# The last group's output leaves in 9 transfers of 128 rows instead of 16 of 64, in a fused linear-attention and SwiGLU kernel

## The chip, the cores and the metric

The kernel runs on one core of a Trainium2 chip. The metric is the device time of one execution in microseconds, as the median of several runs; before the change it was 297.41 us, the median of three runs that lay between 297.12 and 297.60. The same inputs are used each time. Matrices are float32 in memory, multiplied as float16 and summed in float32.

## What is computed

The input is linear attention with 8 batches, 8 heads, 576 positions and 64 dimensions per head; its result is taken as 4608 tokens of 512 numbers each and goes through a gated feed-forward layer of width 1536.

```python
def _attn_ref(q, k, v):                       # each (8, 8, 576, 64)
    def phi(x):
        return np.where(x > 0, x, np.exp(x) - 1.0) + 1.0
    q_p, k_p = (phi(q), phi(k))
    kv = np.einsum('bhsd,bhse->bhde', k_p, v)
    z = np.sum(k_p, axis=2)
    num = np.einsum('bhsd,bhde->bhse', q_p, kv)
    den = np.einsum('bhsd,bhd->bhs', q_p, z)[..., None] + 1e-06
    return (num / den).astype(np.float32)

def _moe_ref(x, w_gate, w_val, w_out):        # x (4608, 512), w_gate and w_val (512, 1536), w_out (1536, 512)
    g = x @ w_gate
    silu = g * (1.0 / (1.0 + np.exp(-g)))
    val = x @ w_val
    return (silu * val @ w_out).astype(np.float32)
```

Between the two, x is attn_out.transpose(0, 2, 1, 3) reshaped to (4608, 512).

## The kernel before

**Groups and tokens.** The 4608 tokens are worked off in 9 groups of 512, g = 0 to 8. A group is 8 units of 64 tokens. A unit (b, j) holds the positions 9c + j of batch b, for c = 0 to 63; so the rows of one unit lie 9 rows apart in `out`, and two units j and j + 1 lie beside each other. The last group, g = 8, is batch 7 with j = 1 to 8. A partition of an output tile is a token: the tile `osb[2 * th + tt]` holds two units, one in partitions 0 to 63 and one in 64 to 127. There are four such tiles, (th, tt) in {0, 1} x {0, 1}; below, `o0.0`, `o1.0`, `o2.1` and so on mean `osb` tile and column half (256 of the 512 columns).

**Layer 1** (lines 351 to 380) makes `hT`, the hidden activations in float16, on TensorE (PE), with ScalarE (ACT) for copies and Silu and VectorE (DVE) for products. **Layer 2** multiplies `hT` by `w_out`. From group 1 on, both use a scheme with seven block products in place of eight. In layer 2 each half tt of a group's tokens has the products 1 to 7, each 6 matmuls of 128 x 128 by 256 columns (`prd`, L456, line of the matmul). Sums of `hT` that products 3, 5, 6 and 7 need are made by DVE (`h_sum`, L425, tiles `hs`). The results are put together out of PSUM by `keep` (ACT, L465, PSUM to `part`), `copy_half` (ACT, L461) and `fin` (DVE, L470: PSUM times a constant plus `part`, into `osb`). Of one half tt, with o1 = `osb[tt]` and o2 = `osb[2 + tt]`:

- product 1 goes to bank x, and `keep` takes it to `part0`; product 2 goes to bank z, and `fin` makes the left columns of o1;
- product 6 is added in x and kept in `part1`; product 5 is added in z and kept in `part2`;
- product 7 is added in x, and `fin` with `part2` makes the right columns of o2;
- product 3 is added in z, and `fin` with `part1` makes the right columns of o1;
- product 4 is added in x, and a copy makes the left columns of o2. For the last group's tt = 1 this copy is a `tensor_scalar` on DVE (L997).

Bank x is `pX[tt]`, bank z is `(pX[2], pV[2])[tt]`. `seed_bank(tt)` is `(pV[1], pG[1])[tt]`, a bank that layer 1 uses; a switch `SEED[g]`, false for all groups, could send product 2 there.

**The order of the work.** For groups 1 to 8 nothing is issued where it is written. `op(engine, cost, function, reads, writes)` records an operation, `ORDER[g]` gives the order of the layer 2 products of a group ("51e" is product 5 of tt = 1, its first five matmuls; "51d" the sixth), and at the end a list of numbers written out in full decides the order in which all recorded operations are issued (an engine works off its own operations in that order):

```python
    for i in steps.split():
        ops[int(i)][2]()
```

The second argument of `op` is a planner's cost and has no effect on the device.

**The output.** Groups 1 to 7 write whole rows: `put` issues two transfers per tile on the queue of SyncE (SP), each 64 rows of 2 KB. The last group writes each column half as soon as it is done, `out_op` with two transfers of `put_1` (L1014), one per unit: 64 rows of 1 KB, that is 64 KB. These are 16 transfers: 13 issued by SP, 2 by ACT and 1 by GpSimd (POOL). The DRAM side of `put_1` picks one j, so it is 64 rows that lie 9 rows apart; the on-chip side is 64 partitions.

Of the kernel before, what the change touches and what calls it, by code (L numbers as in the profile page):

```python
# [13 lines left out]
P = 128  # L14
# [3 lines left out]
def kernel(  # L18
# [414 lines left out]
    def l2_banks(tt):  # L433
        return (pX[0], pX[1])[tt], (pX[2], pV[2])[tt]
# [4 lines left out]
    def prd(g, n, tt, fs, seeded):  # L439
# [15 lines left out]
        for (i, f) in enumerate(fs):  # L455
            nc.tensor.matmul(out=(z if n in (2, 3, 5) else x)[:, 0:HD], lhsT=left(f), rhs=right(f),  # L456
                             start=(i == 0 and fs[0] == 0 and (n in (1, 5) or n == 2 and not seeded)),
                             stop=(i == len(fs) - 1), skip_group_check=True)
# [9 lines left out]
    def fin(tt, th, ch, i, from_x):  # L468
        (x, z) = l2_banks(tt)
        nc.vector.scalar_tensor_tensor(out=osb[2 * th + tt][:, HD * ch:HD * ch + HD],  # L470
                                       in0=(x if from_x else z)[:, 0:HD], scalar=1.0 / SC, in1=part[:, 2 * i + tt, :],
                                       op0=ALU.mult, op1=ALU.add)
# [484 lines left out]
    def l2_prd(g, n, tt, fs=tuple(range(HF)), done=True):  # L957
# [11 lines left out]
        if n == 1:  # L969
            if sd:  # L970
                op("ACT", 0.3, lambda: copy_half(x, seed_bank(tt)[:, 0:HD], 1.0), [nm(x)], [nm(seed_bank(tt))])
            else:
                op("ACT", 0.3, lambda: keep(tt, 0, True), [nm(x)], [f"part0{tt}"])
        if n == 2:
            if sd:
                op("ACT", 0.3, lambda: copy_half(dst, o1[:, 0:HD], 1.0 / SC), [nm(dst)], [f"o{tt}.0"])
            else:
                op("DVE", 0.34, lambda: fin(tt, 0, 0, 0, False), [nm(z), f"part0{tt}"], [f"o{tt}.0"])
# [6 lines left out]
        if n == 7:  # L985
            op("DVE", 0.34, lambda: fin(tt, 1, 1, 2, True), [nm(x), f"part2{tt}"], [f"o{2 + tt}.1"])
            if last:
                out_op(g, tt, 1, 1, (nc.sync, nc.scalar) if tt else (nc.sync, nc.sync))
        if n == 3:
            op("DVE", 0.34, lambda: fin(tt, 0, 1, 1, False), [nm(z), f"part1{tt}"], [f"o{tt}.1"])  # L990
            if last:
                out_op(g, tt, 0, 1, (nc.sync, nc.gpsimd) if tt else (nc.sync, nc.sync))
            else:
                op("SP", 0.12, lambda: put(g, tt, 0), [f"o{tt}.0", f"o{tt}.1"], [])
        if n == 4:
            if last and tt:
                op("DVE", 0.34, lambda: nc.vector.tensor_scalar(out=o2[:, 0:HD], in0=x[:, 0:HD], scalar1=1.0 / SC, scalar2=None,  # L997
                                                                op0=ALU.mult), [nm(x)], [f"o{2 + tt}.0"])
                out_op(g, tt, 1, 0, (nc.sync, nc.scalar))
# [7 lines left out]
    def out_op(g, tt, th, ch, engs=(nc.sync, nc.sync)):  # L1007
        for e in range(2):
            eng = {id(nc.sync): "SP", id(nc.scalar): "ACT", id(nc.gpsimd): "POOL"}[id(engs[e])]
            op(eng, 0.06, lambda e=e: put_1(g, tt, th, ch, e, engs[e]), [f"o{2 * th + tt}.{ch}"], [])  # L1010

    def put_1(g, tt, th, ch, e, eng):
        (b, j) = units(g)[2 * (2 * th + tt) + e]
        eng.dma_start(out=out[S * b:S * b + S, HD * ch:HD * ch + HD].rearrange("(c j) f -> j c f", j=J)[j],  # L1014
                      in_=osb[2 * th + tt][C * e:C * e + C, HD * ch:HD * ch + HD])
# [122 lines left out]

    def program():
# [21 lines left out]
        0 1 4 14 15 9 17 18 10 5 20 21 23 6 24 26 27 16 29 3 19 30 32 8 2 33 35 36 7 22 38 28 41 25 39 40 42 31  # L1161
        34 44 45 43 37 47 63 46 48 64 49 105 66 12 50 67 69 106 65 70 51 11 72 68 73 52 75 71 13 76 114 78 77 79
        74 81 80 82 84 53 83 85 54 87 86 88 90 55 89 91 107 93 56 94 92 96 95 57 97 99 98 100 58 102 59 101 103
        113 127 104 60 129 108 128 109 131 117 171 133 110 132 130 135 112 115 137 134 139 111 136 125 138 120
        141 116 143 119 142 145 140 118 122 147 146 144 150 124 126 148 153 121 162 151 156 61 165 155 154 123
        168 62 149 152 163 167 158 176 164 157 172 177 169 159 179 166 170 178 160 181 161 197 180 342 199 182
        200 343 183 198 202 184 204 201 206 203 174 207 185 209 208 205 211 186 210 214 215 173 212 218 220 219
        213 222 175 221 187 223 225 216 224 227 217 229 228 188 230 285 226 232 231 189 234 236 235 237 233 240
        242 238 241 245 243 246 239 248 190 247 250 244 249 252 251 253 276 255 191 254 257 256 259 277 192 258
        193 260 262 261 264 194 267 265 268 263 271 266 273 269 272 274 270 284 298 275 300 278 280 299 302 279  # L1170
        301 286 281 304 303 282 306 288 308 305 287 310 307 296 309 289 312 283 314 313 311 316 290 291 318 317
        315 293 321 319 324 322 297 292 333 326 336 294 325 334 195 339 327 328 347 329 196 320 348 504 323 340
        335 338 350 330 341 337 349 331 352 368 332 353 370 354 369 371 355 373 372 375 356 295 377 357 378 380
        379 376 382 381 358 385 386 351 383 389 344 387 391 393 390 392 394 374 384 396 359 398 397 388 400 360
        399 401 395 403 456 405 402 404 407 345 408 406 411 409 413 346 412 361 416 410 414 417 419 415 418 421
        364 423 422 424 420 426 425 362 428 430 429 447 431 363 365 448 427 433 432 435 438 436 439 434 442 437
        444 440 443 445 441 455 469 446 471 449 470 450 473 457 451 475 452 474 472 477 459 476 479 453 478 481
        467 480 454 462 483 458 485 484 460 487 482 464 486 489 488 498 461 491 501 490 366 468 492 505 499 493
        367 507 494 500 506 496 510 508 495 512 466 502 463 515 503 509 517 497 513 465 516 523 514 518 525 519
        511 527 529 524 528 540 526 542 541 545 543 531 547 546 629 550 530 552 548 551 554 532 553 556 544 558  # L1180
        555 561 557 559 563 562 549 566 560 564 568 567 570 565 569 533 572 571 574 573 577 620 579 575 578 582
        580 576 584 534 586 583 588 585 587 590 589 593 581 591 595 594 598 621 521 600 596 602 601 603 599 535
        606 592 604 608 607 611 597 605 612 609 520 614 613 615 536 617 616 522 618 628 610 642 537 619 644 622
        643 624 646 632 623 648 625 626 645 650 635 647 652 649 627 654 651 653 637 656 633 658 634 657 660 655
        700 630 662 661 671 659 663 640 631 674 664 672 641 666 667 677 665 675 679 636 678 682 668 680 684 639
        669 670 687 638 689 688 701 694 538 685 691 696 690 702 683 539 698 673 676 681 686 706 695 703 715 697
        699 717 716 704 720 707 722 721 725 718 708 705 727 726 723 729 728 731 709 719 733 730 736 732 734 738
        737 724 741 739 743 742 745 710 804 744 747 735 749 746 752 748 750 754 753 740 757 755 751 759 758 761
        711 756 763 760 762 765 764 768 712 770 766 769 773 713 693 775 771 777 714 778 767 776 781 774 779 783
        782 772 786 780 784 787 692 789 797 788 790 792 798 791 793 785 803 815 795 794 817 796 816 819 799 807  # L1190
        800 821 820 801 818 823 805 825 822 802 827 824 826 810 829 808 831 871 830 806 833 828 812 832 835 834
        844 872 836 809 847 837 845 838 873 850 846 839 852 840 848 851 855 841 849 853 842 857 814 843 854 860
        874 862 811 861 865 858 875 864 867 813 859 863 856 869 876 882 866 891 870 868 893 892 877 896 894 884
        898 897 901 880 883 903 902 905 895 899 907 904 909 906 908 900 912 910 914 913 917 885 911 915 919 918
        921 886 916 923 920 887 922 925 924 928 878 930 929 933 926 879 881 935 934 931 937 936 888 939 927 938
        941 944 940 889 932 946 890 945 942 949 951 947 950 953 979 952 955 954 943 957 960 980 956 962 948 961
        958 965 968 963 959 969 966 971 972 970 967 974 964 973 975 977 978 981 976 989 990 991 992 993 983 996
        982 998 1000 997 1002 984 1004 999 985 1011 994 1003 1006 1001 1013 988 995 1015 987 1014 1007 1017 1012
        1016 986 1005 1019 1047 1018 1021 1008 1020 1023 1009 1022 1026 1024 1028 1010 1027 1025 1048 1031 1029
        1033 1049 1032 1030 1036 1034 1050 1038 1037 1035 1051 1041 1039 1052 1043 1042 1040 1045 1053 1044 1060  # L1200
        1046 1062 1061 1065 1056 1067 1066 1070 1063 1072 1068 1071 1074 1073 1054 1076 1064 1078 1075 1055 1057
        1081 1077 1079 1083 1082 1069 1086 1080 1084 1088 1087 1090 1058 1092 1089 1094 1091 1093 1059 1097 1095
        1099 1098 1085 1102 1096 1100 1104 1103 1106 1101 1108 1105 1107 1110 1109 1148 1113 1111 1115 1114 1118
# [43 lines left out]
```

## Time and profile before

The profile is of one execution of this kernel. Its own time was 297.82 us; the span from the first to the last record is 296.0 us, and 1.82 us lie around it.

| What | Value |
|---|---|
| median of three runs | 297.41 us (297.12 to 297.60) |
| profiled execution, span | 297.82 us, 296.0 us |
| PE busy | 286.4 us, 97% |
| DVE busy | 258.6 us, 87% |
| ACT busy | 236.3 us, 80% |
| POOL busy | 42.5 us, 14% |
| granted PE clock | 0.998 |
| last matmul of the program starts | 289.76 us |
| last copy out of PSUM | 290.07 to 290.49 us |
| last output issue on SP starts | 292.65 us |
| last output transfer has landed | 294.66 us |
| end of the span | 296.0 us |

How to read it: times are microseconds from the start of the span. PE, DVE, ACT and POOL are engines with their busy time; PEld is TensorE's loading of weights, which runs beside its matmuls. A line of the timeline gives start, duration, engine, line of the kernel, operation, output and inputs, shape and how many; instructions that follow each other closely are drawn together, so the duration is that of the group. SPq, ACTq and POOLq are the instructions of an engine that issue transfers; they aren't counted as busy. A bracket at the end of a line gives idle time before it and what ended it. In the DMA view a queue's line gives packets, megabytes and the time that the packets took, as a share of 16 DMA engines over the window; a transfer's line gives where from and to, who issued it, how many, the size of one and the median time from issue to landing.

### The profile page before, as it was taken

Reading aid. Unit: us, or ns where it says so; the run is one execution under the profiler, and the core shown is the slowest. Engines: PE = TensorE matmul, PEld = TensorE weight load, DVE = VectorE, ACT = ScalarE, POOL = GpSimd, SP = SyncE. Lnnn points to the kernel's source line nnn. Section 1 sums busy time; section 2 is a strip of 40 time slices with the busy share of each in tenths; the row PEclk is TensorE's granted clock in tenths of the full one; section 3 lists DMA queues with packets and bytes.
Section 4 is the critical chain, followed back from the end, with each engine's and each line's share of the span. In section 5 each row is a group of like instructions: output and inputs, shape, how many; then the busy total and the mean of one; then the engine's idle time right before and its main releaser. Section 6 shows DMA issues by size and latency. Waiting matters only on the chain.

```text
span 296.0 us, 7377 instructions
## 1 busy us (share of the span) xinstructions
PE 286.4 (97%) x2939; PEld 212.9 (72%) x2939; DVE 258.6 (87%) x521; ACT 236.3 (80%) x405; POOL 42.5 (14%) x55
## 2 busy tenths in 40 slices
PE   7899999999999999999999999999999999999991
PEld 5644454454866687668887888788888888788881
DVE  4667889999999998999899999999999999757961
ACT  4773977983998689969999999999986688668830
POOL 8554436500000011000100010000000000000000
PEclk9999999999999999999999999999999999999999
DMA  7999999995598319661960669304140443050014
GB/s 203 193 196 200 205 207 207 196 216 87 81 171 190 64 15 171 162 105 33 147 181 2 105 98 222 61 2 100 44 73 2 99 95 22 2 129 15 0 41 103
DMA packets 41506, 32.92 MB, mean 111 GB/s; under 512 B 16432, under 2 KB 36848, under 8 KB 41472
## 3 DMA queue, kind: packets, MB, share of 16 engines
q0 software_dynamic: 20176, 18.35, 40.7%
q1 hardware_dynamic: 21136, 13.97, 21.0%
q8 instruction: 23, 0.38, 0.5%
q10 hardware_dynamic: 160, 0.13, 0.2%
q14 instruction: 11, 0.09, 0.1%
HBM read 37.75 MB, written 9.44 MB: 159 GB/s over the span
## 4 chain that ended last, share of the span: by engine, by line
issue 50%; PE 43%; DMA 2%; ACT 2%; POOL 1%; POOLq 0%
PE pV L826 7%; PE pX L456 6%; PE pG L826 6%; PE pX L351 5%; PE pX L297 3%; PE pV L297 3%; DMA q<-in_q_dram 2%; PE pG L383 2%; PE pV L383 2%; PE pG L297 2%; PE pV L456 2%; PE pX L826 1%; PE pX L268 1%; PE pV L351 1%; PE pX L187 1%
## 5 line engine op out<-in xcount | busy, mean ns | idle before, releaser
L351 PEld LDWEIGHTS <-wl 128*128 128x128 f16 x414 | 40.3, 98 | 9.6 <-issue 0.2
L456 PEld LDWEIGHTS <-hs 128*128 128x128 f16 x384 | 37.2, 98 | 5.4 <-issue 0.7
L456 PEld LDWEIGHTS <-hT 128*128 128x128 f16 x288 | 27.7, 98 | 5.1 <-DVE hs L425 0.4
L351 PEld LDWEIGHTS <-wg 128*128 128x128 f16 x272 | 26.4, 98 | 5.7
L456 PE MATMUL pX<-ws,hs 128*128 128x256 f16 x240 | 28.8, 273 | 0.1
L826 PE MATMUL pV<-xt,wv 128*128 128x512 f16 x104 | 28.3, 379 | 0.0
L368 ACT ACTIVATE ek<-eq 128x512 f16<-128x512 f32 x34 | 21.3, 625 | 5.3 <-DVE eq L855 5.2
L351 PE MATMUL pV<-xt,wg 128*128 128x256 f16 x168 | 23.9, 273 | 0.0
L826 PE MATMUL pG<-xt,wg 128*128 128x512 f16 x80 | 22.5, 379 | 0.0
L368 ACT ACTIVATE ek<-pV 128x512 f16<-128x512 f32 x34 | 20.3, 597 | 2.7 <-PE pV L351 1.9
L351 PE MATMUL pX<-xs,wl 128*128 128x256 f16 x132 | 19.8, 273 | 0.0
L465 ACT ACTIVATE part<-pX 128x256 f32<-128x256 f32 x40 | 14.3, 386 | 6.4 <-PE pX L456 6.3
L456 PE MATMUL pX<-wo,hT 128*128 128x256 f16 x144 | 19.0, 273 | 0.0
L371 DVE SCALAR_TENSOR_TENSOR r<-pG,rr 128x512 f16<-128x512 f32 x20 | 13.7, 687 | 5.5 <-PE pG L351 5.2
L374 DVE SCALAR_TENSOR_TENSOR hT<-pV,sil 128x512 f16<-128x512 f32 x26 | 17.6, 684 | 0.9 <-PE pV L826 0.3
L425 DVE TENSOR_TENSOR hs<-hT 128x512 f16<-128x512 f16 (+3 forms) x35 | 17.8, 514 | 0.0
L365 ACT ACTIVATE rr<-pX 128x512 f32<-128x512 f32 x27 | 15.9, 598 | 2.4 <-PE pX L351 2.3
L470 DVE SCALAR_TENSOR_TENSOR osb<-pX,part 128x256 f32<-128x256 f32 x32 | 12.9, 419 | 5.2 <-ACT part L465 2.9
L1014 POOL DMA_DIRECT2D out_dram<-osb x1 | 0.6, 562 | 116.8 <-DVE osb L470 116.8
L249 DVE TENSOR_TENSOR qp<-qp,rden 128x768 f16<-128x768 f16 (+3 forms) x19 | 17.2, 906 | 0.0
L826 PEld LDWEIGHTS <-wv 128*128 128x128 f16 x112 | 10.9, 98 | 8.5
L124 ACT ACTIVATE ek<-k 128x1152 f16<-128x1152 f16 x14 | 16.1, 1161 | 1.3 <-DMA k<-in_k_dram 1.3
(187 smaller groups left out, 725.2 us busy)
## 6 DMA issues: line engine op xcount, KB each, us to landing
out_dram<-osb SPq DMA_DIRECT2D x64, 128.0 KB, 2.9
k<-in_k_dram POOLq DMA_DIRECT2D x7, 576.0 KB, 7.4
q<-in_q_dram POOLq DMA_DIRECT2D x7, 576.0 KB, 8.9
v<-in_v_dram POOLq DMA_DIRECT2D x7, 576.0 KB, 6.3
wg<-in_moe_w_gate_dram POOLq DMA_DIRECT2D x5, 256.0 KB, 9.2
wv<-in_moe_w_val_dram POOLq DMA_DIRECT2D x5, 256.0 KB, 9.8
wo<-in_moe_w_out_dram POOLq DMA_DIRECT2D x2, 512.0 KB, 15.1
out_dram<-osb SPq DMA_DIRECT2D x13, 64.0 KB, 2.1
```

What stands on the lines that cost most here:

```text
L124: nc.scalar.activation(out=e[:, s, :], in_=src[ix(b)][:, s, :], func=AF.Exp, bias=0.0, scale=1.0)
L249: nc.vector.tensor_tensor(out=qv, in0=qv, in1=rden[:, HL * j0:HL * j1].unsqueeze(2).to_broadcast([P, HL * (j1 - j0), D]), op=ALU.mult)
L297: nc.tensor.matmul(out=ps[:, :], lhsT=src[:, i, P * fb:P * fb + P], rhs=xT[i][g % 2][:, :], start=(i == 0), stop=(i == 3))
L351: nc.tensor.matmul(out=dst[:, HN * e:HN * e + HN], lhsT=lhs, rhs=rhs, start=(n in (1, 5) and e == 0 and c == 0), stop=(c == 1), skip_group ...
L365: nc.scalar.activation(out=dst, in_=halves(src), func=AF.Copy, bias=0.0, scale=scale)
L368: nc.scalar.activation(out=dst, in_=src, func=AF.Silu, bias=0.0, scale=1.0)
L371: nc.vector.scalar_tensor_tensor(out=dst, in0=halves(src), scalar=SC, in1=b, op0=ALU.mult, op1=op1)
L374: nc.vector.scalar_tensor_tensor(out=hT[:, fb, :], in0=pv[:, :], scalar=SC, in1=s[:, :], op0=ALU.mult, op1=ALU.mult)
L425: (eng or nc.vector).tensor_tensor(out=o, in0=a, in1=b, op=op)
L456: nc.tensor.matmul(out=(z if n in (2, 3, 5) else x)[:, 0:HD], lhsT=left(f), rhs=right(f), start=(i == 0 and fs[0] == 0 and (n in (1, 5) or ...
L465: nc.scalar.activation(out=part[:, 2 * i + tt, :], in_=(x if from_x else z)[:, 0:HD], func=AF.Copy, bias=0.0, scale=1.0 / SC)
L826: nc.tensor.matmul(out=dst[:, :], lhsT=src[:, i, P * fb:P * fb + P], rhs=xT[i][g % 2][:, :], start=(i == 0), stop=(i == 3))
```

## The change

The change touches the end of layer 2 and the order of the work.

1. **Transfers.** The eight column halves of the last group are now written with one transfer each of both units, 128 partitions, in place of two of 64; the DRAM side picks two neighbouring j, so it is 2 times 64 rows. Only the last, the left half of `osb[3]`, is written in two transfers of 128 columns (512 B a row). That makes 9: seven on SP, two on ACT (`o3.1` and the second part of `o3.0`), none on POOL.
2. **The last copy** (product 4 of tt = 1) is split: DVE copies the first 128 columns, ACT the other 128, and each half has its own transfer, DVE's on SP and ACT's on ACT.
3. **The last group's products** come in another order (`ORDER[8]`), and with `SEED[8] = 2` product 2 goes to the bank `seed_bank(tt)`, from which `fin(own=True)` reads it; there is no copy of product 1 into that bank.
4. **The list `steps`** is replaced as a whole. PE's operations are the same up to the 490th of 507 (509 after). Of DVE's 421 operations 243 stand at another place in its own order, of ACT's 358 (359 after) 129, over all groups. SP's order differs only in the last group, and the loads are as before.

```diff
             nc.tensor.matmul(out=(z if n in (2, 3, 5) else x)[:, 0:HD], lhsT=left(f), rhs=right(f),
-                             start=(i == 0 and fs[0] == 0 and (n in (1, 5) or n == 2 and not seeded)),
+                             start=(i == 0 and fs[0] == 0 and (n in (1, 5) or n == 2 and seeded is not True)),
...
-    def fin(tt, th, ch, i, from_x):
+    def fin(tt, th, ch, i, from_x, own=False):
         (x, z) = l2_banks(tt)
+        if own:
+            z = seed_bank(tt)
...
         if n == 1:
-            if sd:
+            if sd is True:
...
         if n == 2:
-            if sd:
+            if sd is True:
...
-                op("DVE", 0.34, lambda: fin(tt, 0, 0, 0, False), [nm(z), f"part0{tt}"], [f"o{tt}.0"])
+                op("DVE", 0.34, lambda: fin(tt, 0, 0, 0, False, sd == 2), [nm(dst), f"part0{tt}"], [f"o{tt}.0"])
...
-                out_op(g, tt, 1, 1, (nc.sync, nc.scalar) if tt else (nc.sync, nc.sync))
+                out_op(g, tt, 1, 1)
...
-                out_op(g, tt, 0, 1, (nc.sync, nc.gpsimd) if tt else (nc.sync, nc.sync))
+                out_op(g, tt, 0, 1)
...
         if n == 4:
             if last and tt:
-                op("DVE", 0.34, lambda: nc.vector.tensor_scalar(out=o2[:, 0:HD], in0=x[:, 0:HD], scalar1=1.0 / SC, scalar2=None,
-                                                                op0=ALU.mult), [nm(x)], [f"o{2 + tt}.0"])
-                out_op(g, tt, 1, 0, (nc.sync, nc.scalar))
+                hd = HD // 2
+                op("DVE", 0.2, lambda: nc.vector.tensor_scalar(out=o2[:, 0:hd], in0=x[:, 0:hd], scalar1=1.0 / SC, scalar2=None,
+                                                               op0=ALU.mult), [nm(x)], [f"o{2 + tt}.0a"])
+                op("ACT", 0.2, lambda: nc.scalar.activation(out=o2[:, hd:HD], in_=x[:, hd:HD], func=AF.Copy, bias=0.0,
+                                                            scale=1.0 / SC), [nm(x)], [f"o{2 + tt}.0b"])
+                op("SP", 0.06, lambda: put_1(g, tt, 1, 0, 0, 2, nc.sync, 0, hd), [f"o{2 + tt}.0a"], [])
+                op("ACT", 0.06, lambda: put_1(g, tt, 1, 0, 0, 2, nc.scalar, hd, HD), [f"o{2 + tt}.0b"], [])
...
-    def put_1(g, tt, th, ch, e, eng):
-        (b, j) = units(g)[2 * (2 * th + tt) + e]
-        eng.dma_start(out=out[S * b:S * b + S, HD * ch:HD * ch + HD].rearrange("(c j) f -> j c f", j=J)[j],
-                      in_=osb[2 * th + tt][C * e:C * e + C, HD * ch:HD * ch + HD])
+    OUTQ = {(0, 0, 0): "S", (0, 0, 1): "S", (1, 1, 0): "S", (0, 1, 0): "S", (1, 0, 0): "S", (1, 1, 1): "A", (0, 1, 1): "S"}
+    QUEUE = {"S": ("SP", nc.sync), "A": ("ACT", nc.scalar), "P": ("POOL", nc.gpsimd)}
+
+    def out_op(g, tt, th, ch):
+        qs = OUTQ[(th, ch, tt)]
+        for (i, x) in enumerate(qs):
+            e0, e1 = (0, 2) if len(qs) == 1 else (i, i + 1)
+            op(QUEUE[x][0], 0.06, lambda x=x, e0=e0, e1=e1: put_1(g, tt, th, ch, e0, e1, QUEUE[x][1]), [f"o{2 * th + tt}.{ch}"], [])
+
+    def put_1(g, tt, th, ch, e0, e1, eng, c0=0, c1=HD):
+        (b, j) = units(g)[2 * (2 * th + tt) + e0]
+        eng.dma_start(out=out[S * b:S * b + S, HD * ch + c0:HD * ch + c1].rearrange("(c j) f -> j c f", j=J)[j:j + e1 - e0],
+                      in_=osb[2 * th + tt][C * e0:C * e1, HD * ch + c0:HD * ch + c1])
...
-    ORDER[8] = "10c 20c 11c 21c 10d 20d 11d 21d 60 61 50 70 30 40 51 71 31 41"
+    ORDER[8] = "10c 11c 20c 21c 10d 11d 50e 20d 21d 60 61 51e 50d 51d 70 71 30 40 31 41"; SEED[8] = 2
```

## The prediction

> **What bounds the kernel now.** I read the page first, then the timeline of the last 15 us, the queue of SP (SyncE) alone, the waits, and the DMA view in small windows.
>
> ```profile
> span 296.0 us, 7377 instructions
> ...
> PE 286.4 (97%) x2939; PEld 212.9 (72%) x2939; DVE 258.6 (87%) x521; ACT 236.3 (80%) x405; POOL 42.5 (14%) x55
> ```
>
> TensorE (PE) is busy for 286.4 of 296.0 us, and from group 1 on its matmuls follow each other at their own length. So VectorE (DVE) and ScalarE (ACT) cost nothing while PE never waits for them. What is left is the tail. Timeline of 281 to 296 us (start, duration, engine, line):
>
> ```profile
> 282.76 0.27 PE L456 MATMUL pV<-wo,hT 128*128 128x256 f16 x1
> 283.17 2.78 PE L456 MATMUL pX<-ws,hs 128*128 128x256 f16 x24
> ...
> 283.80 9.40 SPq L1014 DMA_DIRECT2D out_dram<-osb  x13
> ...
> 285.79 0.82 PE L456 MATMUL pX<-wo,hs 128*128 128x256 f16 x6
> ...
> 286.52 0.81 PE L456 MATMUL pX<-ws,hT 128*128 128x256 f16 x6
> ...
> 290.07 0.42 DVE L997 TENSOR_SCALAR osb<-pX 128x256 f32<-128x256 f32 x1 [0.31 <-PE pX L456]
> ```
>
> 24 matmuls in 2.78 us, the last 0.27 long, are 0.109 apart. From 282.76 to 283.17 is 0.41: a stall of 0.30. Six start at 285.79, so the next was due at 286.44 and came at 286.52: 0.08, and the same again at 289.22 (after 288.49). PE loses 0.46 in the tail. The last copy ends at 290.49, and then SP still has a backlog:
>
> ```profile
> 289.85 3.36 SPq L1014 DMA_DIRECT2D out_dram<-osb  x5
> ```
>
> ```profile
> 292.02 1.19 SPq L1014 DMA_DIRECT2D out_dram<-osb  x2
> ```
>
> These are two windows of the same queue, from 289.8 and from 292.1 us: five issues fill 289.85 to 293.21, and the last starts at 292.65 (293.21 less 0.55), 2.16 after its data. The DMA view of 283 to 296 us (packets, MB, share of 16 engines; then issues, size, median time to landing):
>
> ```profile
> q1 hardware_dynamic: 1040, 0.85, 29.0%
> ...
> out_dram<-osb SPq DMA_DIRECT2D x13, 64.0 KB, 2.1
> ```
>
> The last issue lands 2.0 later, at 294.66; SP's final semaphore waits and drains take 1.33 more, to 296.0. The profiled execution took 297.82, the median of three runs is 297.41. Changes of the span are added to the median; about 0.6 us (0.2%) is what a measurement tells from no change.
>
> **The copies and products (small).** The reordered list puts the first five matmuls of product 5 between the last matmuls of products 1 and 2, and gives products 3 and 4 of a half at least one other product after the `fin` that frees their bank: the three stalls go, −0.46, next late is nothing on PE. Product 2 now goes to a seed bank, whose last reader is the Silu at 280.61 to 281.19; the product starts at 281.12 but that Silu now runs ahead of its neighbour, so I cost it at nothing, 0.07 without that cover. The last copy takes 0.42 for 256 columns; 512 columns take 0.684 (L371), so 128 take about 0.29 (ACT, 0.384 and 0.597: 0.28): −0.13. Both halves read one PSUM bank; no row shows two engines reading one bank together, so ACT's half costs 0 to 0.29 more. The ACT-issued transfer of `o3.1` waits for `fin` of product 7; ACT's next copies queue behind it, but that `fin` ends about 1 us before the copy of product 4 could start.
>
> **The planner's order (groups 1 to 8).** PE's order is the same up to its 490th operation of 507; of 421 DVE operations 243 stand elsewhere, of ACT's 129 of 358. For each I summed the trace durations of what moved ahead of it, less what moved behind, and set this against the time from its end to its PE user's start. 19 places overrun, by 5.5 us in all; that is the upper end. The lower is −0.33, PE's stalls there beyond a fixed 0.09 at each change of matmul shape; the largest:
>
> ```profile
> 211.62 0.60 PE L351 MATMUL pV<-xs,wl 128*128 128x256 f16 x4
> 211.63 0.31 PEld L351 LDWEIGHTS <-wl 128*128 128x128 f16 x3 [0.23 <-issue]
> ```
>
> It waits for the ACT copy at 210.99, now moved ahead of the Silu at 210.47, so −0.22. Overruns mostly vanish when walked, as here in group 8:
>
> ```profile
> 269.99 0.60 ACT L368 ACTIVATE ek<-pV 128x512 f16<-128x512 f32 x1 [0.33 <-PE pV L351]
> 270.62 0.58 ACT L365 ACTIVATE pV<-pG 128x512 f32<-128x512 f32 x1
> 271.12 0.62 ACT L368 ACTIVATE ek<-eq 128x512 f16<-128x512 f32 x1
> ```
>
> The last one moves ahead of the other two, 0.52 more in front, but ACT idles 0.33 before 269.99 and waits for PE at 270.62: 269.58 + 0.52 + 0.50 is 270.60, no shift. I take −0.22, nearest to this row.
>
> **The transfers (large).** Nine instead of sixteen: SP issues 7, ACT 2, POOL none. Seven move 128 rows of 1 KB, two 128 rows of 512 B. If they spread like today's, SP's issue stays near 0.55 (the page's first loads, 256 rows, issue as fast) and the backlog goes. But the pattern is new: in DRAM a transfer's outermost step is now j, of length 2, with 64 rows inside; it was 64 rows flat. In the DMA view above 1040 packets are 13 times 80: 64 rows and 16 completions, so sixteen engines take four rows each. The first two loads (window 1.5 to 6.0 us) are outermost 128:
>
> ```profile
> q1 hardware_dynamic: 544, 1.18, 75.6%
> ```
>
> 544 is twice 256 rows and 16 completions. So every outermost length that the trace shows is a multiple of 16 and was dealt over 16 engines. No row shows a length of 2. Two ends: 16 engines, 8 rows each; or two slices, two engines, 64 rows each. I take the second: slices of the outermost step are all that the trace shows being dealt out.
>
> The Trainium skill, "DMA: Bandwidth & Descriptors", section "Why a DMA increments its semaphore by 16 and not by 1", speaks against this change: it says the engines used are the largest number up to 16 that divides the slowest dimension of both sides, which would be 2 here; and that a transfer with fewer takes the lowest-numbered ones, so they would queue; by it the two-engine sum below holds, and by a spread over 16 the fast rival's. No run here shows a length of 2 yet.
>
> The price of a row: sixteen engines at once, 29.0% of 16 times 13 us is 60.3 us for 832 rows, 0.072 each. One engine alone (window 287.42 to 287.56, two rows and a completion):
>
> ```profile
> q1 hardware_dynamic: 3, 0.00, 4.6%
> ```
>
> 4.6% of 16 times 0.14 us is 0.103: 0.034 to 0.052 a row. Two engines are nearest to the lone one; a completion carries almost nothing, so 0.048. A full transfer is 64 times 0.048, 3.07 per engine; seven are 21.5. A half-wide one is 1.5 to 3.1, I take 2.3, two are 4.6. Sum 26.1, on the same two engines if a transfer always takes the first ones. DVE finishes `o0.0` 0.80 later than today (behind `o1.0`'s `fin` and an `hs` sum: 284.16 instead of 283.36), so the first issue is at 284.6, and bytes move 1.1 later (283.80 to about 284.95 now): 285.7. Queued work keeps both engines busy from there: 285.7 + 26.1 = 311.8, landing 0.4 later (2.0 less 1.1 and 0.46 of moving), end 1.33 later: span 313.55, +17.55. 297.41 + 17.55 = 315.0. All gains on PE are hidden under this queue. An issue that finds an engine occupied holds its queue (SP, one issue of 1.59 from 285.60), so SP's and ACT's issues should stretch to about 3 us; ACT has two copies behind its first, but nothing that the engines would not serve later anyway.
>
> Ends: 0.034 a row and half of it for half rows gives 17.4, 306.2; 0.072 and full price for half rows gives 41.3, 330.
>
> **Rivals.**
>
> *Faster: sixteen engines.* It decides if a pattern of outermost length 2 is dealt over all sixteen; break-even lies at about six engines: 26.1 on each of two is 52.2 us of engine time, and from 285.7 to 294.26 (today's last landing less 0.4) are 8.6 us. Then the last copy ends at 290.49 − 0.46 − 0.22 − 0.13 = 289.68; SP is held until 289.81 by `o1.1`'s issue (ready 289.16, 0.03 and 0.60); 2.0 and 0.15 for the extra rows per engine (four rows of 0.072 at most) give 291.96 against 294.66: −2.7, 294.7. If issues of 128 rows take double, +1.1: 295.8. For it: every transfer so far used sixteen. Against it: none had this pattern. 0.17.
>
> *Faster, a little: two engines, others each time.* Then the transfers don't queue behind each other, and the last whole one decides: `o1.1`, ready at 289.16, bytes from 290.3 for 3.07, landed 0.4 later, at 293.8 against 294.66: 296.5. Against it: with sixteen of sixteen in every row, nothing shows a rotation. 0.04.
>
> *Two engines at the shared price.* 0.072 a row, up to 330; against it, only two engines draw on memory at once. 0.07.
>
> *New stalls.* Sixteen engines and all overruns real: 294.7 + 0.2 + 5.5 = 300.4. Against it the ACT rows above. 0.03.
>
> *The split does not split.* If ACT's half waits for DVE's, its transfer starts up to 0.29 later: the fast case becomes 294.9. This moves no sign.
>
> **How the numbers follow.** Two engines at 306 to 330: 0.76 (0.07 of it the shared price). Faster: 0.21, sixteen engines (0.17) and the rotation (0.04), 294.3 to 296.5. New stalls that eat the gain: half within 0.2%, half slower, 0.03 together. So faster 0.21, same 0.02, slower 0.77. The likeliest case's own range is 306 to 324. The range must reach the faster case: 294.5 to 320 holds about 0.2 of the fast ones, 0.03 of the stalls and 0.6 of the slow one.
>
> **What would show it.** Per transfer 130 packets (128 and 2 completions) in the two-engine case, 144 for sixteen; the DMA digits after PE's end at 1 (2 of 16) for some 20 us, or at 5 and more for 2 us; landing after many us, or 2.2; SP issues of 3 us, or 0.55. PE's last matmul should start at about 289.1 in either case, unless ACT is held at its issue early enough to stop PE. Wrong would be: 144 packets, an idle DMA tail, or an end that PE sets.

## The result, and the profile after

The changed kernel takes 312.1 us (median of 4 runs, 311.76 to 312.25) against 297.5 us for the kernel before (median of 4 runs, the three from before the change among them): a ratio of 1.049, interval 1.047 to 1.051. The profiled execution took 311.76 us with a span of 309.9 us. The head of its page:

```profile
span 309.9 us, 7365 instructions
...
PE 286.4 (92%) x2939; PEld 213.1 (69%) x2939; DVE 258.8 (84%) x521; ACT 235.6 (76%) x406; POOL 42.7 (14%) x54
```

TensorE is as busy as before, 286.4 us, in a span that is 13.9 us longer: no engine works noticeably more, something is waited for at the end. Two windows of SP's queue in the timeline, from 283 us and from 290.1 us, then 288 to 296 us of the timeline, and ACT's two issues in the view of the line that issues (shortest, median and longest in ns):

```profile
283.87 18.06 SPq L1024 DMA_DIRECT2D out_dram<-osb  x7
```

```profile
290.16 11.77 SPq L1024 DMA_DIRECT2D out_dram<-osb  x3
```

```profile
288.56 0.29 DVE L1000 TENSOR_SCALAR osb<-pX 128x128 f32<-128x128 f32 x1 [0.23 <-PE pX L456]
288.89 0.28 ACT L1002 ACTIVATE osb<-pX 128x128 f32<-128x128 f32 x1 [0.79 <-DVE osb L1000]
289.20 0.53 ACTq L1024 DMA_DIRECT2D out_dram<-osb  x1
```

```profile
L1024 ACTq DMA_DIRECT2D out_dram<-osb x2: 527/832/1137, 286.5 to 289.2; - x2
```

The last copy has ended at 289.17, 1.3 us earlier than before (290.49). But SP, at that moment, is still in its fourth issue; the last three take 11.77 us, 5.08, 3.48 and 3.02 each, where one took 0.55 before. The span ends 20.7 us after the last copy. The DMA view of 283 to 310 us:

```profile
DMA  0101111111111111111111111111111111111000
GB/s 0 24 0 27 35 27 47 47 47 49 41 18 49 49 47 49 49 49 49 47 46 46 47 47 46 47 49 49 47 49 49 49 49 49 49 43 44 28 0 0
...
q1 hardware_dynamic: 910, 0.85, 9.4%
q10 hardware_dynamic: 260, 0.20, 2.4%
```

A digit of 1 stands for 10 to 20% of 16 engines, and two of 16 are 12.5%: two engines for 23 us, at about 48 GB/s. 910 packets on SP's queue are 7 times 130, 260 on ACT's are 2 times 130: 128 rows and 2 completions, where before 80 were 64 rows and 16 completions. The first row starts at 285.08, the last ends at 308.46, the span 1.44 later.

### The profile page after: what moved, and what is told of

Its sections match the earlier page's. It is cut to its first block, busy times and chain, and to the rows that moved or that the text cites. A ratio compares the mean times of both kernels' runs of the same rounds, so it can differ in the third digit from the quotient of the medians.

```text
span 309.9 us, 7365 instructions
## 1 busy us (share of the span) xinstructions
PE 286.4 (92%) x2939; PEld 213.1 (69%) x2939; DVE 258.8 (84%) x521; ACT 235.6 (76%) x406; POOL 42.7 (14%) x54
## 4 chain that ended last, share of the span: by engine, by line
PE 82%; DMA 10%; POOL 1%; issue 0%; DVE 0%; ACT 0%; POOLq 0%
PE pX L456 19%; PE pV L351 13%; PE pG L351 11%; PE pX L351 9%; PE pV L828 8%; PE pG L828 6%; PE pV L456 5%; DMA wo<-in_moe_w_out_dram 4%; DMA wv<-in_moe_w_val_dram 3%; DMA v<-in_v_dram 3%; PE pV L383 2%; PE pG L383 2%; PE pX L828 2%; PE pX L187 1%; PE pG L268 1%; PE pV L268 1%
## 5 line engine op out<-in xcount | busy, mean ns | idle before, releaser
L456 PE MATMUL pX<-wo,hT 128*128 128x256 f16 x138 | 18.2, 273 | 0.0
L351 PE MATMUL pG<-xs,wl 128*128 128x256 f16 x100 | 16.9, 272 | 0.0
L368 ACT ACTIVATE sil<-pG 128x512 f16<-128x512 f32 x20 | 11.9, 593 | 5.4 <-PE pG L828 4.7
```

Of the source, the lines that this page charges most:

```text
L351: nc.tensor.matmul(out=dst[:, HN * e:HN * e + HN], lhsT=lhs, rhs=rhs, start=(n in (1, 5) and e == 0 and c == 0), stop=(c == 1), skip_group ...
L368: nc.scalar.activation(out=dst, in_=src, func=AF.Silu, bias=0.0, scale=1.0)
```

## Experiments

The kernel before was run again beside each set; its medians there were 297.28, 297.54 and 297.13 us.

**The transfers undone, all else kept.**

```diff
-        (b, j) = units(g)[2 * (2 * th + tt) + e0]
-        eng.dma_start(out=out[S * b:S * b + S, HD * ch + c0:HD * ch + c1].rearrange("(c j) f -> j c f", j=J)[j:j + e1 - e0],
-                      in_=osb[2 * th + tt][C * e0:C * e1, HD * ch + c0:HD * ch + c1])
+        for e in range(e0, e1):
+            (b, j) = units(g)[2 * (2 * th + tt) + e]
+            eng.dma_start(out=out[S * b:S * b + S, HD * ch + c0:HD * ch + c1].rearrange("(c j) f -> j c f", j=J)[j],
+                          in_=osb[2 * th + tt][C * e:C * e + C, HD * ch + c0:HD * ch + c1])
```

> The changed kernel with one thing undone: every 128-row transfer is issued as two of 64 rows on the same queue, at the same place (18 transfers: 14 on SP, 4 on ACT). Theory (a DRAM pattern whose outermost length is 2 uses two DMA engines, and that is all of the loss): each transfer shows 64 packets and 16 completions again, SP's issues go back to about 0.55 us, SP issues o0.1 to o3.0a back to back from 287.05 of the changed kernel's profile, eight of them, the last at about 290.9, landed 292.9, end 294.3; that profile began 1.0 us ahead, so 296.7 us, between 295.5 and 297.5. Rival (the reordered list or the split copy costs the time): it stays above 305 us.

Measured: 297.41 us, ratio 1.000 (0.999 to 1.002). The 14.6 us are gone, so order and copies don't cost them. But nothing was won either, though the last copy ended at 289.49. SP's queue in this kernel's timeline from 283 us, and in its DMA view of 283 to 295.7 us:

```profile
284.19 9.24 SPq L1025 DMA_DIRECT2D out_dram<-osb  x14
```

```profile
q1 hardware_dynamic: 1120, 0.85, 29.4%
```

1120 is 14 times 80: sixteen engines again. SP issues without a break from 284.19 to 293.43, 0.66 us per transfer, where the expectation had counted 0.55 and a later start of the backlog. The kernel before left SP at 293.21. So it seems that the queue of issues sets the end in both and hides what PE, VectorE and ScalarE finish earlier; the last two experiments below test that.

**The transfers alone, on the kernel before.** All eight column halves as one transfer of 128 rows on SP.

```diff
-        eng.dma_start(out=out[S * b:S * b + S, HD * ch:HD * ch + HD].rearrange("(c j) f -> j c f", j=J)[j],
-                      in_=osb[2 * th + tt][C * e:C * e + C, HD * ch:HD * ch + HD])
+        if e == 0:
+            eng.dma_start(out=out[S * b:S * b + S, HD * ch:HD * ch + HD].rearrange("(c j) f -> j c f", j=J)[j:j + 2],
+                          in_=osb[2 * th + tt][:, HD * ch:HD * ch + HD])
```

> The kernel before with the one edit alone: each of the last group's eight column halves leaves in one transfer of 128 rows (all eight on SP), order and copies as before. Theory: eight times 128 packets and 2 completions; 8 times 64 rows of 0.046 us on each of two engines are 23.6 us from about 285.0 on, so the last byte at 308.6, the end at 310.0 and 311.4 us, between 309 and 313. Rival (order or split copy): 297.4 us.

Measured: 310.28 us, one run, 13.0 more than the 297.28 beside it. The loss comes with this edit alone. SP's queue from 287 us:

```profile
286.52 12.58 SPq L1015 DMA_DIRECT2D out_dram<-osb  x5
```

The last four issues start 2.67 us apart, about the time that two engines need for one transfer (2.72 from one transfer's last packet to the next one's). Eight transfers moved from 284.43 to 306.86, 22.4 us for 512 rows on each engine, 0.044 a row.

**The same 128 rows with the outermost step made long.** The tokens of the last group are interleaved when ACT writes xT, so that partition 2c + e holds row c of unit e; the DRAM pattern is then 64 times 2 rows.

```diff
+        if g == NG - 1:
+            nc.scalar.activation(out=dst.rearrange("p (t c e) -> p t e c", t=4, e=2),
+                                 in_=ps[i][:, :].rearrange("p (t e c) -> p t e c", t=4, e=2), func=AF.Copy, bias=0.0, scale=1.0 / SC)
...
-.rearrange("(c j) f -> j c f", j=J)[j:j + e1 - e0],
+.rearrange("(c j) f -> c j f", j=J)[:, j:j + 2],
```

> The changed kernel with the same nine transfers of 128 rows, but the tokens of the last group are interleaved (partition 2c+e holds unit e, row c; the four ACT copies into xT of that group write with a stride), so that the DRAM side is 64 times 2 rows and not 2 times 64. Theory (the outermost length decides): 144 packets a transfer, sixteen engines, SP's issues near 0.6 us, last landing 2.1 us after the last issue, end of span at about 293 to 294.5: 295.2 us, between 294.3 and 296.5. Rival (128 rows, or a DRAM pattern of three levels, confine a transfer to two engines however they are ordered): 312 us.

Measured: 294.36 us, ratio 0.991 (0.989 to 0.993); run again later, 294.43 us, 0.991 (0.989 to 0.993). So neither 128 rows nor three levels confine a transfer; what is left is the length of the outermost step. DMA view of 283 to 296 us, and SP's queue in the timeline of 283 to 292 us:

```profile
q1 hardware_dynamic: 1008, 0.85, 19.8%
...
out_dram<-osb SPq DMA_DIRECT2D x6, 128.0 KB, 2.1
```

```profile
284.14 5.67 SPq L1027 DMA_DIRECT2D out_dram<-osb  x7
```

1008 is 7 times 144, 128 rows and 16 completions. SP's issues last 0.54 to 0.61, about as for half the rows, and most of them now wait for data instead of for each other. The four copies into xT that interleave take 0.73 to 0.78 us each, those without it 0.59 to 0.61 in the profile after; PE's stalls around them (253 to 255 us) are the same. This is the change with one step of its pattern turned, and it is faster than both kernels.

**Flat patterns of other lengths.** The kernel before, with only the first 62, 57 or 63 rows of each unit sent.

```diff
-.rearrange("(c j) f -> j c f", j=J)[j],
-                      in_=osb[2 * th + tt][C * e:C * e + C, HD * ch:HD * ch + HD])
+.rearrange("(c j) f -> j c f", j=J)[j][0:62],
+                      in_=osb[2 * th + tt][C * e:C * e + 62, HD * ch:HD * ch + HD])
```

> The kernel before with its 16 flat transfers, but each moves 62 rows of the 64 (two rows of each unit of the last group are left unwritten). No nested pattern, and 62 is 2 times 31. Theory as a divisor (the largest number up to 16 that divides the outermost length): two engines, 62 packets and 2 completions; 16 times 31 rows of 0.046 us are 22.8 us from 285.0: last byte 307.8, 310.6 us, between 308 and 313. Rival (slices of the outermost step are dealt out as evenly as they come, and only a short outermost step hurts): sixteen engines, 62 packets and up to 16 completions, 297.4 us.

> The kernel before with 16 flat transfers of 57 rows of the 64 each (seven rows of each unit of the last group are left unwritten). 57 is 3 times 19. Theory (the largest divisor up to 16): three engines, 57 packets and 3 completions, 19 rows per engine; 16 times 19 rows of 0.046 us are 14.0 us from about 284.5: last byte 298.5 to 299, 301.5 us, between 299.5 and 303.5. Rival (odd or small outermost lengths fall back to one or two engines): 308 us or more.

> The kernel before with 16 flat transfers of 63 rows of the 64 each (one row of each unit of the last group is left unwritten). 63 is 9 times 7. Theory (the largest divisor up to 16): nine engines, 63 packets and 9 completions, seven rows per engine; 16 times 7 rows of 0.046 us are 5.2 us, less than the 8.8 us over which SP issues, so no loss: 297.4 us, between 296.5 and 298. It bears on the prediction's break-even of about six engines. Rival (anything short of sixteen engines delays): 299 us or more.

Measured, one run each: 308.75, 301.21 and 296.48 us, beside 297.28 (for 62) and 297.54 us. SP's 13 transfers in the DMA view, for 62 rows (window 283 to 306 us), 57 rows (283 to 299) and 63 rows (283 to 294):

```profile
q1 hardware_dynamic: 832, 0.83, 10.7%
```

```profile
q1 hardware_dynamic: 780, 0.76, 14.4%
```

```profile
q1 hardware_dynamic: 936, 0.84, 25.4%
```

832 is 13 times 64 (62 rows, 2 completions), 780 is 13 times 60 (57 and 3), 936 is 13 times 72 (63 and 9). A flat pattern without any nesting loses 11.5 us when its length is 62. By the completions, the engines are 2, 3, 9 and, for 64, 16: each time the largest number up to 16 that divides the outermost length. The Trainium skill, "DMA: Bandwidth & Descriptors", section "Why a DMA increments its semaphore by 16 and not by 1", states this rule for the slowest dimension of both sides. These runs agree with it at five lengths (2, 57, 62, 63, 64). With nine engines nothing is lost; with three it is 3.7 us, with 11% fewer rows. That fits the prediction's break-even of about six.

**The last copy whole again.** As c_outer, with one copy by DVE and eight transfers.

```diff
-                hd = HD // 2
...
+                op("DVE", 0.2, lambda: nc.vector.tensor_scalar(out=o2[:, 0:HD], in0=x[:, 0:HD], scalar1=1.0 / SC, scalar2=None,
+                                                               op0=ALU.mult), [nm(x)], [f"o{2 + tt}.0a"])
```

> As c_outer, but the last copy is whole again: DVE copies all 256 columns and SP sends them in one transfer of 128 rows (eight transfers in all). In c_outer's profile ACT's half started only when DVE's had ended (289.15 against 288.83 to 289.12) and its transfer was issued at 289.46. Theory (the split gains nothing because the halves run one after the other): the whole copy ends at 288.83 + 0.42 = 289.25, the issue is at 289.30, 0.16 earlier, the landing of whole rows 0.1 longer: 294.3 us, between 293.9 and 294.7, no difference from c_outer's 294.36 that can be told. Rival (the split brings the 0.13 us that the prediction put down, and a second queue more): 0.2 to 0.7 us slower than c_outer, 294.6 to 295.1 us.

Measured: 294.49 us, ratio 0.990 (0.989 to 0.992). The split is worth nothing that these runs can tell.

**Why the halves run in a row.** As c_outer, but ACT's half goes to a free slot of `part` and leaves from there.

```diff
-                op("ACT", 0.2, lambda: nc.scalar.activation(out=o2[:, hd:HD], in_=x[:, hd:HD], func=AF.Copy, bias=0.0,
+                op("ACT", 0.2, lambda: nc.scalar.activation(out=part[:, 0, 0:hd], in_=x[:, hd:HD], func=AF.Copy, bias=0.0,
```

> As c_outer (nine transfers, interleaved tokens, split last copy), but ACT's half of the last copy goes to another on-chip tile (a free slot of part) and is sent from there. In c_outer ACT's half waits for VectorE's counter and starts 0.03 after DVE's half has ended. Theory A (the two halves are put in a row because both read one PSUM bank): nothing changes, ACT's half starts when DVE's ends, 294.4 us, 294.0 to 294.8. Theory B (because both write one osb tile): both halves start together, ACT's about 0.3 earlier, its issue 0.3 earlier, 294.1 us, 293.7 to 294.5.

Measured: 294.62 us, ratio 0.991 (0.989 to 0.993); the other expectation, of c_outer run again beside it, is this:

> c_outer again, beside split_tile and against the same runs of the kernel before: 294.4 us, 294.0 to 294.8, a ratio of 0.990 with the 2 in 10 thousand that several profiles differ in their first 15 us around it.

The timeline of the kernel with two tiles, 288 to 296 us:

```profile
289.08 0.29 DVE L1003 TENSOR_SCALAR osb<-pX 128x128 f32<-128x128 f32 x1 [0.23 <-PE pX L459]
289.46 0.28 ACT L1005 ACTIVATE part<-pX 128x128 f32<-128x128 f32 x1 [1.31 <-DVE osb L1003]
```

ACT waits for DVE's half although they no longer share a destination, as theory A had it. What they still share is the PSUM bank. The wait is a semaphore in the program, so the run doesn't show what the hardware would do without it; that wasn't tried.

**What the reordered list is worth.** The kernel before, its order and its whole copy, with interleaved tokens and eight transfers of 128 rows (the two edits of c_outer and only128 together).

> The kernel before (its order, its whole last copy) with the last group's tokens interleaved as in c_outer and eight transfers of 128 rows on SP. It shows what the reordered list is worth once the queue is out of the way. Theory (the reorder takes away 0.46 of stalls in the tail and 0.22 at 211.62, which the backlog hid): SP is not behind, the last copy ends 0.7 us later than in c_outer_one, and so does the span: 295.0 us, between 294.4 and 295.7. Rival (transfers alone made c_outer's gain): the same as c_outer, 294.0 to 294.4 us.

Measured: 295.28 us, ratio 0.992 (0.991 to 0.994). Its profile still has the three stalls of the tail (0.31, 0.08, 0.08) and the 0.22 of mid-kernel, which c_outer's and c_outer_one's profiles lack. These 0.7 are near the 0.8 us between its median and c_outer_one's, from the same set, but the two intervals (0.991 to 0.994, 0.989 to 0.992) overlap, so the size of the difference isn't secured. The traces give less: from 60 us to the last matmul, PE takes 0.6 less in c_outer_one than here, and in c_outer only 0.36, since there a new stall of 0.21 stands at 78.5 us. Of the 3 us that the kernels with both gain, the transfers alone bring 2.3.

The same run also gives the price of a row on sixteen engines with 128 rows a transfer (DMA view of 283 to 299 us):

```profile
q1 hardware_dynamic: 1152, 1.05, 19.6%
```

19.6% of 16 times 16 us is 50 us for 1024 rows, 0.049 each. So the 0.072 that the prediction read from the kernel before isn't the price of sharing memory among sixteen engines; it goes with transfers of 64 rows on sixteen engines (0.070 in rows64 too), and why isn't known.

**64 rows, on two queues.** As rows64, the second of each pair issued by ACT.

```diff
-            eng.dma_start(
+            (nc.sync, nc.scalar)[e].dma_start(
```

> As rows64 (transfers of 64 rows, sixteen engines each, no interleaving), but of each pair of transfers the first is issued by SP and the second by ACT: nine issues on each queue in place of 14 and 4. rows64 ended with SP's issues back to back from 286.18 to 293.44. Theory (the time of rows64 is SP's backlog of issues, and the reorder's gain lies hidden under it): SP's last issue comes 2 us or more earlier, ACT's last at about 290.5 (after its half copy and with two issues to go), the landing at 292.6, 295.5 us, between 294.6 and 296.5; ACT's issues between its copies may hold a copy and stall PE, which is the upper end. Rival (the backlog isn't the cause, the transfers themselves take the time): 297.4 us.

Measured: 296.53 us, ratio 0.998 (0.997 to 0.999): faster than the kernel before, as rows64 was not, and SP's last issue starts at 291.43 where it started at 292.84; that speaks for the backlog. The time is just outside the expected 294.6 to 296.5, a miss by 0.03. ACT's part of the timeline from 288.5 us:

```profile
289.09 1.38 ACTq L1025 DMA_DIRECT2D out_dram<-osb  x2
290.57 0.28 ACT L1002 ACTIVATE osb<-pX 128x128 f32<-128x128 f32 x1 [1.51 <-issue]
```

ACT's half of the last copy starts at 290.57, 1.65 after DVE's (288.92): it stands behind two issues in ACT's own queue. PE has no stall in this tail; the cost fell on the copy, not on PE as the expectation put it.

## Why the prediction was right

**The forecast case came.** Two engines, 130 packets a transfer, a digit of 1 and SP's issues of 3 us and more: each was named beforehand and each is in the profile. ACT's issues, which were to stretch to about 3 us as well, took 1.14 and 0.53. 312.1 us against 315.0, inside 306 to 330 for this case. What decided it was the choice between the two ends of a cost that no row of the kernel before showed. The argument from the trace, that slices of the outermost step are dealt out and two slices so go to two engines, gave the right number partly by luck: 62 slices went to two engines too, so the rule is the divisor, and at length 2 both readings give two.

**The terms of the sum.** By spans, 313.55 was put down and 309.9 came, 3.65 less. The drain was put at 26.1 and took 23.4 us (285.08 to 308.46). Once it runs steadily, a full transfer takes 2.71 (from 304.23 to 306.94) and not 3.07, so a row costs each of the two engines 0.042 instead of 0.048; that is 2.5 over seven full transfers. A half-wide transfer took 1.55 on its own (306.90 to 308.45), not 2.3, 1.5 for two. Slower rows in the first 8 us gave 1.3 back (over all of only128 a row is 0.044). The first byte came 0.6 earlier than put down. The end followed the last byte by 1.44, not 1.73. The lone engine's packets were the right row to take; their mean length overstated the price a little, because packets of one engine overlap: the two rows of that window start 0.044 apart and last 0.046 to 0.048.

**PE.** The three stalls of the tail went (0.47, put at 0.46), the one at 211.62 too (0.22 as put), and of the 5.5 us of 19 overruns next to nothing appeared: 0.07 at 191 us, and in five of the six other profiles with this list (not in c_outer_one's) one stall of 0.17 to 0.21 at 78.5 us. The walk along idle times was the right reading, but for these. The last matmul started at 288.26, not at 289.1. The rest comes from the start: matmul for matmul, this profile is 1.1 us ahead of the profile before at 15 us, and 0.85 still at 205 us. The other profiles are 0.2 to 1.0 ahead at 15 us, those of the kernels with the old order too, so it isn't the change. All of it was hidden, as said.

**What was off.** The split was booked at −0.13 with a bound of 0.29 for the shared bank; its rival "the split does not split" is what happened: [0.79 <-DVE] in the profile after, and no gain over c_outer_one. The two halves together took 0.61 (288.56 to 289.17) where the whole copy took 0.42, so the term was +0.19 and not −0.13. The fast rival's number, 294.7, is close to what sixteen engines gave (294.36), but that takes a pattern that this change doesn't have.

**What hid the gain.** rows64 shows a thing that the prediction had only half: with sixteen engines and 64 rows the reorder gains nothing, since SP's issues, one every 0.66 to 0.67 us in the backlog, end at 293.2 without it and at 293.4 with it. Fewer transfers were the right aim.

## What to carry to other kernels

Before merging transfers, look at the length of the outermost step on both sides: 64 rows in one step went to 16 engines, two steps of 64 rows to two engines. If the data can be laid out so that the long index is outermost (here in four copies that were there anyway, 0.16 us longer each and off PE's path), then the new order with 8 or 9 transfers of 128 rows is 3 us faster than 16 of 64, 2.3 of it by the transfers; otherwise the smaller ones are better. For transfers that SP or ACT issued, count packets against rows in the DMA view: what is left over per transfer is the number of engines that took part.

## What the runs showed of the hardware

An issue from SP took 0.54 to 0.61 us with 128 rows on sixteen engines and mostly 0.47 to 0.59 with 64, but with flat patterns of 63 and 57 rows, on nine and three engines, mostly 0.24 to 0.34 (the last one of flat63, from 290.32 us, 0.28). The number of engines alone doesn't set it: with 62 rows on two engines an issue took 0.24 to 0.44 before SP fell behind, but the first three of the changed kernel, 2 times 64 rows on two engines, took 0.51 to 0.61. What sets it stays open, and whether a queue bound by its issues gains from fewer engines wasn't tested: flat63's 296.48 us are one run with 63 of 64 rows.

SP could run only so far ahead of two engines, and that is what stretched its issues. In only128, from the fourth on, an issue ended 0.4 to 0.6 us after the last packet of the transfer three before it (the fifth at 291.07, after 290.56); with 62 rows, from the seventh to the tenth, 0.16 after that of the transfer five before it (the eighth at 289.45, after 289.29).

Transfers that ACT issued shared the two engines of SP's: on q10 the rows of `o3.1` began only at 290.05, although its issue started at 286.46, and the DMA digit stayed at 1 while both queues moved rows.
